# A kernel of attention and two MLPs: stores of weights behind their uses, an order made with traced durations, earlier conversions of weights

## The chip, the cores and the metric

One core of a Trainium2 chip. The time is that of one execution on the device, in microseconds (us); the median of some runs is given with the lowest and the highest. The profile is of one execution and has its own time. The engines are called PE (TensorE, the matrix products; PEld is its loading of weights), DVE (VectorE), ACT (ScalarE), POOL (GpSimd) and SP (SyncE, whose queue issues the DMAs).

## The reference

Three parts follow one another on 4 x 576 = 2304 rows of 512 numbers:

```python
# attention with a window of 128, 8 heads of 64
scores = scale * q @ k.T;  scores = where(mask, scores + bias, -1e9)
x = softmax(scores) @ v                                  # 2304 x 512
# mixing of tokens, then of channels (d_ch = 1536)
h  = maximum(xt @ w_tok1, 0) @ w_tok2;   u = x + h.T     # xt: x with rows and columns exchanged, per batch
x  = u + maximum(u @ w_ch1, 0) @ w_ch2
# normalization and a second mixing of channels (2048)
xn = (x - mu) / sqrt(var + 1e-6) * g_ln
out = x + maximum(xn @ w_ch1, 0) @ w_ch2
```

The four matrices of the channel MLPs are float64 in memory (`wa1`, `wa2` of the first, `wb1`, `wb2` of the second).

## The kernel before

The rows are 18 tiles of 128. Attention runs over the tiles, two calls a tile (`n` = 0 to 35 counts them); the token MLP is fed in between (`later()`), and so are loads of weights: while `n` lies from `W_START` on in steps of `W_STEP`, a call brings one weight of channel layer 0 (n = 24, 27, 30 and 33), and the rest of the first six come right behind attention. Then channel layer 0 and channel layer 1 follow, as 42 steps, each a layer, a chunk of tiles (tiles 0 to 7, then 16 and 17, then 8 to 15) and a pair of weight tiles of 128 x 512.

A weight is converted on the chip (`load_f64`, line 377): two DMAs of 512 KB bring it (`rh`, `rw`, line 400), ACT makes `e` (line 412), and DVE takes four instructions for it: `s` (lines 415 and 417), `m` (419), and the float32 result `w` or `y` (427). A list `uses` holds every use of a weight in turn; use number k, weight k below, has a tile `w` from a ring of `W_BUFS` = 6. A weight that is used again later, by another chunk, is stored as float32 in memory (`keep_w`, line 478; the store has line 480) and comes back by a load (line 490). Weights of layer 1 are converted ahead into two tiles `y` and stored (`stage_w`).

A product in nearly full float32 is three matmuls: each operand is split in a high part and a low part (`w1h`, `w1l`, `xh`, `xl`, and so on), of which high by high, low by high and high by low are added up. ACT makes the high part, DVE or POOL the low part (line 370). A step on eight tiles makes seven products of blocks from sums of weights and inputs (`w1_of`, `seven_products`; `st` are the sums, `b0` to `b3` the banks of PSUM, lines 971 to 973 the matmuls). ACT takes the positive part `hh` of a bank (line 906), DVE the low part `hl` (line 908), and after that the bank is free for the next step. `second` multiplies by the second weight (`w2h`, `w2l`, lines 1026 to 1028, into `acc`) and DVE adds the result to `u` (line 1031). In the first chunk `w2_of` also stores both parts of the second weight (line 945), the other chunks load them (line 950).

Nothing of this is emitted in the order in which it is written. Every operation is recorded in a `Plan` with its cost on each engine that can do it, what it reads and what it writes. `Plan.order` (line 205) then places the operations one after the other: each engine takes, of what is ready by the costs, what has the lowest rank, and an operation that DVE or POOL can do goes to the one that would end it sooner. Ranks come from the recorded order of the products. Each engine, and SP's queue of DMAs, executes what it was given in that order, so a cost changes the order of all engines and the engine of some operations. The costs are functions of the elements in a row:

```python
def dve(n, fast=False):
    return 68 + n / (1.92 if fast else 0.96)
def pool_tt(n):
    return 149 + 2.1 * n
```

Of the kernel before, what the change touches and what calls it, by code (L numbers as in the profile page):

```python
# [10 lines left out]
F32 = mybir.dt.float32  # L11
# [25 lines left out]
W_BUFS = 6  # L37
# [6 lines left out]

STAGE_RATES = {(0, 2): 2, (1, 0): 2}
WARM, WARM_NS = 10, 320
WT_SHIFT, WT_START, WT_STEP, SHIFT_AT, W_START, W_STEP = 0, 2, 1, 7, 24, 3
SIGN16, EXP16 = 0x80008000 - (1 << 32), 0x7F807F80


# [52 lines left out]
class Plan:  # L103
# [29 lines left out]
        ring.append(b)  # L133
        return b

    def op(self, cost, emit, reads=(), writes=()):
        k = len(self.ops)
        deps, behind = set(), set()
        for group, write in ((reads, False), (writes, True)):
            for x in group:  # L140
                b, key = x if isinstance(x, tuple) else (x, None)
                if not b.ops:
                    if b.pool in self.ctl:
                        b.first.add(self.ctl[b.pool])
                    for a in b.after:
                        assert a.ops, "a ring's tile is not in use yet"
                        a.closed = True
                        b.first.update(a.ops)
                deps.update(b.first)
                if b.behind:  # L150
                    behind.add(b.behind.ops[0])
                assert not getattr(b, "closed", False), f"{b.spec[2]} is used after its place was given away"
                assert write or any(w for key2, (w, _) in b.track.items() if key is None or key2 in (None, key)), \
                    f"{b.spec[2]} is read before it is written"
                b.ops.append(k)
                for key2, (ws, rs) in b.track.items():
                    if key is None or key2 is None or key == key2:
                        deps.update(ws)
                        if write:
                            deps.update(rs)  # L160
                ws, rs = b.track.setdefault(key, ([], []))
                if write:
                    if key is None:
                        b.track = {None: ([k], [])}
                    else:
                        b.track[key] = ([k], [])
                else:
                    rs.append(k)
        deps.discard(k)
        behind.discard(k)  # L170
        self.ops.append((cost, emit, deps, behind - deps, self.shift))
        return k
# [117 lines left out]
    def emit(self):  # L290
        for k in self.order():
            self.ops[k][1](self.taken[k])


def dve(n, fast=False):
    return 68 + n / (1.92 if fast else 0.96)


def act(n, psum=False, pointers=0):
    return (51 if psum else 93) + 0.833 * n + 93 * pointers  # L300


def pool_tt(n):
    return 149 + 2.1 * n


def pool_ts(n):
    return 162 + 0.833 * n


def pe(n):
# [3 lines left out]
def block_kernel(tc, qT, kT, v, wt1, wt2, wa1, wa2, wb1, wb2, g, bias, out):  # L315
    nc = tc.nc
    NF1, NF2 = FF1 // P, FF2 // P
    pl = Plan()
    buf = pl.buf

    def op(cost, emit, reads=(), writes=()):
        return pl.op(cost, (lambda e: emit()) if len(cost) == 1 else emit, reads, writes)

    ENGINE = {"DVE": nc.vector, "POOL": nc.gpsimd}

# [51 lines left out]
    def load_f64(src, k, n, dst=None, get=None):  # L377
# [29 lines left out]
        def half(x):  # L407
# [4 lines left out]
        op({"ACT": act(n)}, lambda: nc.scalar.activation(  # L412
            out=e.t[:, :n], in_=head(BF16), func=AF.Copy, scale=2.0 ** -116), [rh], [e])

        op({"DVE": dve(n // 2, True)}, lambda: nc.vector.tensor_scalar(  # L415
            half(s), half(e), 3, EXP16, ALU.logical_shift_left, ALU.bitwise_and), [e], [s])
        op({"DVE": dve(n // 2)}, lambda: nc.vector.scalar_tensor_tensor(
            out=half(s), in0=half(e), scalar=SIGN16, in1=half(s), op0=ALU.bitwise_and, op1=ALU.bitwise_or), [e], [s])
        op({"DVE": dve(n, True)}, lambda: nc.vector.tensor_scalar(
            m.t[:, :n], rw.t[:, :n, 0], 4, None, ALU.logical_shift_left), [rw], [m])  # L420
        if dst is None:
            dst = y = buf("cvt", [P, DM], F32, "y", 2)
# [1 line left out]
            def get():  # L424
                return y.t[:, :n]

        op({"DVE": dve(n)}, lambda: nc.vector.scalar_tensor_tensor(
            out=get(), in0=m.t[:, :n], scalar=2.0 ** 32, in1=s.t[:, :n], op0=ALU.add, op1=ALU.mult), [m, s], [dst])
        return dst, get

# [18 lines left out]
    uses = []  # L449
# [4 lines left out]
                if m == 1 or steps[j][1] == 0:  # L454
                    uses += [("ab"[steps[j][0]] + str(m), 2 * steps[j][3] + i) for i in range(2)]
    last_use = {x: k for k, x in enumerate(uses)}
    to_stage = [x for k, x in enumerate(uses) if x[0][0] == "b" and x not in uses[:k]]
    src = {"a1": wa1, "a2": wa2, "b1": wb1, "b2": wb2}
    wtiles, staged = [], {}
    used = [0]  # L460
# [14 lines left out]
        pl.op({"DVE": dve(DM), "POOL": pool_tt(DM)}, scale, [y, g_sb], [dst])  # L475
        return dst, get

    def keep_w(x, w, get):
        d = staged[x] = buf("dram", [P, DM], F32, f"d{len(staged)}")
        op({"DMA": 728}, lambda: nc.sync.dma_start(out=d.t, in_=get()), [w], [d])  # L480

    def load_w(upto):

        while len(wtiles) < min(upto, len(uses)):
            k = len(wtiles)
            x = uses[k]
            w = buf("wa", [P, DM], F32, "w", W_BUFS)
            wtiles.append(w)
            if x in staged:
                op({"DMA": 728}, lambda w=w, d=staged[x]: nc.sync.dma_start(out=w.t, in_=d.t), [staged[x]], [w])  # L490
            else:
                convert_w(x, w, lambda w=w: w.t)
                if last_use[x] > k:
                    keep_w(x, w, lambda w=w: w.t)

    def stage_w(n):

# [7 lines left out]
    def take_w():  # L505
        used[0] += 1
        return wtiles[used[0] - 1]


    bias_sb = buf("att", [P, 4, H, P], BF16, "bias_sb")  # L510
# [223 lines left out]
    def attention():  # L734
# [37 lines left out]
        for i in range(-1, NTILE + 1):  # L772
# [15 lines left out]
            for c in range(2):  # L788
# [13 lines left out]
                if n == SHIFT_AT:  # L802
                    shift_wt1()
                if W_START <= n < 2 * NTILE and (n - W_START) % W_STEP == 0:
                    load_w(min(W_BUFS, len(wtiles) + 1))
                later()
        return tok_later

# [92 lines left out]
    def hidden():  # L901
        return [buf("mlq", [P, CW], F32R, "h" + p, H_BUFS) for p in "hl"]

    def relu_to(h, key, c, o, go, n):
        hh, hl = h
        op({"ACT": act(n, True)}, lambda: nc.scalar.activation(  # L906
            out=hh.t[:, c], in_=go(), func=AF.Relu), [o], [(hh, key)])
        op({"DVE": dve(n)}, lambda: nc.vector.scalar_tensor_tensor(  # L908
            out=hl.t[:, c], in0=go(), scalar=0.0, in1=hh.t[:, c].bitcast(F32),
            op0=ALU.max, op1=ALU.subtract), [o, (hh, key)], [(hl, key)])  # L910

    def w1_of(s):

        f1, f2 = take_w(), take_w()
        if len(steps[s][2]) == 2:
            return [w_split("w1", W1_BUFS, x) for x in (f1, f2)]
        a, b = (buf("mlp", [P, DM], F32, "st", ST_BUFS) for _ in range(2))

        def left(x):
# [2 lines left out]
        def right(x):  # L922
            return lambda: x.t[:, HW:]
# [6 lines left out]
        minus((b, 1), right(b), f1, right(f1), (a, 0), left(a), HW)  # L930
        w2 = w_split("w1", W1_BUFS, b)
        w3 = w_split("w1", W1_BUFS, f2, right(f2), HW)
        return [(w0, 0), (w1, 0), (w2, 0), (w1, HW), (w0, HW), (w3, 0), (w2, HW)]

    parts2 = {}

    def w2_of(s):
        out = []
        layer, c, _, n = steps[s]
        for f in (2 * n, 2 * n + 1):  # L940
            if c == 0:
                x = w_split("w2", W2_BUFS, take_w())
                for p, y in zip("hl", x):
                    d = parts2[layer, f, p] = buf("dram", [P, DM], F32, f"d2{layer}{f}{p}")
                    op({"DMA": 728}, lambda d=d, y=y: nc.sync.dma_start(out=d.t, in_=y.t.bitcast(F32)), [y], [d])
            else:
                x = []
                for p in "hl":
# [234 lines left out]
```

## Time and profile before

| | us |
|---|---|
| median of 3 runs (lowest to highest) | 877.15 (875.05 to 880.37) |
| the profiled execution's own time | 875.87 |
| its span | 874.1 |
| PE, PEld busy | 838.7, 686.5 |
| DVE, ACT, POOL busy | 675.1, 367.1, 308.4 |

The span is the time from the first to the last instruction that the profile has. Busy times of different engines overlap. A wait is put down to the instruction that ended last of those that were waited for. The granted clock (PEclk) is 1.00 where PE has 2.4 GHz and 0.5 where it has 1.2. Attention and the token MLP take the first 171 us, channel layer 0 runs to some 446 us, layer 1 from there on.

### The profile page before, as it was taken

How to read it: one execution, taken by the hardware profiler on the slowest of the kernel's cores; microseconds unless marked ns; L12 is line 12 of the kernel's file. 1: busy time of each engine (PE TensorE's matmuls, PEld its weight loads, DVE VectorE, ACT ScalarE, POOL GpSimd, SP SyncE). 2: the span in 40 equal slices, each digit the busy share in tenths (PEclk: the TensorE clock that was granted, in tenths of full speed). 3: DMA queues.
4: the chain of work that ended last, by engine and by line, in shares of the span. 5: the costliest groups of instructions: out<-in, count | busy, mean ns of one | idle time of the engine just before them, and what ended most of it. 6: DMA issues, size and time to landing. Idle time of an engine off the chain costs nothing.

```text
span 874.1 us, 13184 instructions
## 1 busy us (share of the span) xinstructions
PE 838.7 (96%) x4478; PEld 686.5 (79%) x4478; DVE 675.1 (77%) x1406; ACT 367.1 (42%) x880; POOL 308.4 (35%) x327
## 2 busy tenths in 40 slices
PE   7999999969999999999998999999999999999997
PEld 6767787758887788788875787787878988888886
DVE  5787775798888999978799967899678855555554
ACT  6888765533344436223344422433344322222220
POOL 2783545363212456321223434452144322221110
PEclk9999999979999999999999999999999999999999
DMA  8688843057767789987753132885357772221112
GB/s 287 198 232 228 282 137 111 24 172 246 236 222 237 269 282 323 338 278 255 276 189 121 61 128 67 301 294 198 132 169 231 227 230 84 73 72 49 49 49 96
DMA packets 72547, 162.88 MB, mean 186 GB/s; under 512 B 8224, under 2 KB 8352, under 8 KB 72480
## 3 DMA queue, kind: packets, MB, share of 16 engines
q1 hardware_dynamic: 72000, 160.73, 55.4%
q0 software_dynamic: 480, 1.31, 0.8%
q8 instruction: 35, 0.57, 0.3%
q14 instruction: 32, 0.26, 0.1%
HBM read 129.76 MB, written 30.93 MB: 184 GB/s over the span
## 4 chain that ended last, share of the span: by engine, by line
PE 65%; DVE 11%; issue 2%; ACT 1%; POOL 0%; DVEq 0%; POOLq 0%; ACTq 0%
PE acc L1026 11%; PE acc L1028 11%; PE acc L1027 11%; PE b L971 9%; PE b L973 9%; PE b L972 9%; DVE st L824 2%; DVE u L1031 2%; DVE st L370 2%; PE b L436 1%; PE b L438 1%; DVE hl L908 1%; PE b L437 1%; PE p L832 1%; DVE s L415 1%
## 5 line engine op out<-in xcount | busy, mean ns | idle before, releaser
L1031 DVE TENSOR_TENSOR u<-acc,u 128x512 f32<-128x512 f32 x252 | 172.1, 685 | 57.3 <-PE acc L1028 55.8
L1026 PE MATMUL acc<-w2h,hh 128*128 128x512 f32 x504 | 199.2, 395 | 5.8 <-DVE u L1031 5.1
L906 ACT ACTIVATE hh<-b 128x512 fp32r<-128x512 f32 (+1 forms) x140 | 74.4, 553 | 298.2 <-PE b L973 252.9
L1028 PE MATMUL acc<-w2h,hl 128*128 128x512 f32 x504 | 196.8, 390 | 0.8 <-DVE hl L908 0.7
L1027 PE MATMUL acc<-w2l,hh 128*128 128x512 f32 x504 | 196.6, 390 | 0.0
L971 PE MATMUL b<-xh,w1h 128*128 128x512 f32 x392 | 155.7, 397 | 8.6 <-DVE hl L908 5.0
L973 PE MATMUL b<-xh,w1l 128*128 128x512 f32 x392 | 154.1, 393 | 0.6 <-POOL w1l L370 0.6
L972 PE MATMUL b<-xl,w1h 128*128 128x512 f32 x392 | 154.1, 393 | 0.0
L908 DVE SCALAR_TENSOR_TENSOR hl<-b,hh 128x512 fp32r<-128x512 f32 (+1 forms) x140 | 85.6, 630 | 53.2 <-ACT hh L906 52.9
L370 POOL TENSOR_TENSOR w1l<-w,w1h 128x512 fp32r<-128x512 f32 (+1 forms) x47 | 60.8, 1296 | 184.5 <-ACT w1h L357 184.3
L1026 PEld LDWEIGHTS acc<-w2h,hh 128*128 128x128 f32 x504 | 94.7, 188 | 29.6 <-DVE u L1031 10.3
L1028 PEld LDWEIGHTS acc<-w2h,hl 128*128 128x128 f32 x504 | 94.6, 188 | 22.3 <-DVE hl L908 2.4
L1027 PEld LDWEIGHTS acc<-w2l,hh 128*128 128x128 f32 x504 | 94.8, 188 | 18.1
L971 PEld LDWEIGHTS b<-xh,w1h 128*128 128x128 f32 x392 | 74.5, 190 | 26.5 <-DVE hl L908 5.4
L973 PEld LDWEIGHTS b<-xh,w1l 128*128 128x128 f32 x392 | 74.5, 190 | 17.1 <-POOL w1l L370 1.1
L972 PEld LDWEIGHTS b<-xl,w1h 128*128 128x128 f32 x392 | 74.6, 190 | 15.2
L370 POOL TENSOR_TENSOR w1l<-st,w1h 128x512 fp32r<-128x512 f32 x30 | 39.8, 1328 | 125.7 <-ACT w1h L357 118.1
L412 ACT ACTIVATE e<-rh 128x512 bf16<-128x512 bf16 (+2 forms) x65 | 41.2, 634 | 66.0 <-DMA rh<-wb 38.0
L635 ACT ACTIVATE pr<-t,mn 128x128 f32<-128x128 f32 x144 | 55.8, 391 | 19.2 <-DVE mn L626 18.8
L652 POOL TENSOR_SCALAR_AFFINE_SELECT pf<-pf 128x512 f32<-128x512 f32 x64 | 42.8, 671 | 34.1 <-ACT pf L357 32.1
L370 DVE TENSOR_TENSOR b<-b,p 128x512 f32<-128x512 f32 x56 | 38.8, 694 | 18.2 <-PE b L973 18.2
L370 POOL TENSOR_TENSOR xl<-st,xh 128x512 fp32r<-128x512 f32 x23 | 30.0, 1307 | 51.8 <-ACT xh L357 51.7
(118 smaller groups left out, 1371.3 us busy)
## 6 DMA issues: line engine op xcount, KB each, us to landing
w<-d SPq DMA_DIRECT2D x82, 256.0 KB, 3.2
rw<-wb SPq DMA_DIRECT2D x32, 512.0 KB, 4.7
rh<-wb SPq DMA_DIRECT2D x32, 512.0 KB, 4.9
rw<-wa SPq DMA_DIRECT2D x24, 512.0 KB, 4.4
rh<-wa SPq DMA_DIRECT2D x24, 512.0 KB, 4.4
d<-y SPq DMA_DIRECT2D x26, 256.0 KB, 3.9
keys<-kT SPq DMA_DIRECT2D x18, 256.0 KB, 4.1
q<-qT SPq DMA_DIRECT2D x18, 256.0 KB, 4.5
```

The lines of the kernel that those rows point to most:

```text
L370: pl.op({e: cost[e] for e in on}, lambda e: ENGINE[e].tensor_tensor(get(), ga(), gb(), alu), [*several(a), *several(b), *also], several(dst))
L635: op({"ACT": 580}, lambda m=m: nc.scalar.activation(out=pr.t[:, m], in_=t.t[:, m], func=AF.Exp, bias=mn.t[:, m:m + 1], scale=-1.0, accum_o ...
L652: op({"POOL": 630}, lambda a=a: nc.gpsimd.affine_select(pf.t[:, a], pf.t[:, 1], [[0, 4], [1 - 2 * a, P]], (ALU.is_ge, ALU.is_gt)[a], 0.0, ...
L906: op({"ACT": act(n, True)}, lambda: nc.scalar.activation(out=hh.t[:, c], in_=go(), func=AF.Relu), [o], [(hh, key)])
L908: op({"DVE": dve(n)}, lambda: nc.vector.scalar_tensor_tensor(out=hl.t[:, c], in0=go(), scalar=0.0, in1=hh.t[:, c].bitcast(F32), op0=ALU.ma ...
L971: nc.tensor.matmul(g.t, wh.t[:, w], xh.t, start=start and k == 0, stop=False, skip_group_check=True)
L972: nc.tensor.matmul(g.t, wh.t[:, w], xl.t, start=False, stop=False, skip_group_check=True)
L973: nc.tensor.matmul(g.t, wl.t[:, w], xh.t, start=False, stop=stop and k == 1, skip_group_check=True)
L1026: nc.tensor.matmul(o.t, hh.t[:, c:c + P], wh.t, start=j == 0, stop=False)
L1027: nc.tensor.matmul(o.t, hh.t[:, c:c + P], wl.t, start=False, stop=False)
L1028: nc.tensor.matmul(o.t, hl.t[:, c:c + P], wh.t, start=False, stop=j == 1)
L1031: op({"DVE": dve(DM)}, lambda o=o, i=i: nc.vector.tensor_tensor(u[i].t, o.t, u[i].t, ALU.add), [o], [u[i]])
```

## The change

Four things are done. The constants `W_START`, `W_STEP` go from 24, 3 to 18, 2: nine calls in attention (n = 18, 20, to 34) instead of four; the first six load a weight each, the other three stage one (weights 6, 7 and 8, converted into a tile `y`, stored as `d0`, `d1`, `d2` and loaded back later). The store of a loaded weight is recorded no longer with its conversion but behind the splits that use it (`keep_taken`), and it may not stand ahead of the last of these in the order (`behind`). The stores of the parts of the second weight are put behind the last `hl` that was recorded before (`mark`). And the costs of DVE, ACT and POOL are raised; those of the four DVE instructions of a conversion have a factor of 1.3 besides. The rest of the diff passes `behind` on.

```diff
-WT_SHIFT, WT_START, WT_STEP, SHIFT_AT, W_START, W_STEP = 0, 2, 1, 7, 24, 3
+WT_SHIFT, WT_START, WT_STEP, SHIFT_AT, W_START, W_STEP = 0, 2, 1, 7, 18, 2
...
-    def op(self, cost, emit, reads=(), writes=()):
+    def op(self, cost, emit, reads=(), writes=(), behind=()):
         k = len(self.ops)
-        deps, behind = set(), set()
+        deps, behind = set(behind), set()
...
 def dve(n, fast=False):
-    return 68 + n / (1.92 if fast else 0.96)
+    return 150 + n / (1.92 if fast else 0.97)
...
 def act(n, psum=False, pointers=0):
-    return (51 if psum else 93) + 0.833 * n + 93 * pointers
+    return 170 + (0.82 if psum else 0.9) * n + 93 * pointers
...
 def pool_tt(n):
-    return 149 + 2.1 * n
+    return 150 + 2.4 * n
...
 def pool_ts(n):
-    return 162 + 0.833 * n
+    return 200 + 0.95 * n
...
-        op({"DVE": dve(n // 2, True)}, lambda: nc.vector.tensor_scalar(
+        op({"DVE": 1.3 * dve(n // 2, True)}, lambda: nc.vector.tensor_scalar(
             half(s), half(e), 3, EXP16, ALU.logical_shift_left, ALU.bitwise_and), [e], [s])
...
-    to_stage = [x for k, x in enumerate(uses) if x[0][0] == "b" and x not in uses[:k]]
+    to_stage = [x for k, x in enumerate(uses) if x not in uses[:k]]
...
-    def keep_w(x, w, get):
+    def keep_w(x, w, get, behind=()):
         d = staged[x] = buf("dram", [P, DM], F32, f"d{len(staged)}")
-        op({"DMA": 728}, lambda: nc.sync.dma_start(out=d.t, in_=get()), [w], [d])
+        op({"DMA": 728}, lambda: nc.sync.dma_start(out=d.t, in_=get()), [w], [d], behind)
...
                 convert_w(x, w, lambda w=w: w.t)
-                if last_use[x] > k:
-                    keep_w(x, w, lambda w=w: w.t)
...
+    def keep_taken(n):
+
+        for k in range(used[0] - n, used[0]):
+            if uses[k] not in staged and last_use[uses[k]] > k:
+                keep_w(uses[k], wtiles[k], lambda w=wtiles[k]: w.t, [len(pl.ops) - 1])
...
                 if W_START <= n < 2 * NTILE and (n - W_START) % W_STEP == 0:
-                    load_w(min(W_BUFS, len(wtiles) + 1))
+                    if len(wtiles) < W_BUFS:
+                        load_w(len(wtiles) + 1)
+                    else:
+                        stage_w(1)
...
-        op({"DVE": dve(n)}, lambda: nc.vector.scalar_tensor_tensor(
+        mark[0] = op({"DVE": dve(n)}, lambda: nc.vector.scalar_tensor_tensor(
...
         w3 = w_split("w1", W1_BUFS, f2, right(f2), HW)
+        keep_taken(2)
...
         layer, c, _, n = steps[s]
+        last = [mark[0]]
...
-                    op({"DMA": 728}, lambda d=d, y=y: nc.sync.dma_start(out=d.t, in_=y.t.bitcast(F32)), [y], [d])
+                    op({"DMA": 728}, lambda d=d, y=y: nc.sync.dma_start(out=d.t, in_=y.t.bitcast(F32)), [y], [d], last)
```

Lines up to 490 keep their numbers; behind that line 908 becomes 918, 945 becomes 959, 971 to 973 become 985 to 987, 1026 to 1028 become 1040 to 1042 and 1031 becomes 1045. In the order that comes out, 36 operations go from DVE to POOL. The numbers behind a name below tell one instance of a buffer from another.

On DVE, the last instructions ahead of the first `hl` of channel layer 0 (`hl` frees bank `b0`; `e`, `s`, `m`, `rw` belong to conversions), before:

```order
L415 TENSOR_SCALAR s_2468<-e_2215 128x256
L419 TENSOR_SCALAR m_2476<-rw_2012 128x512
L417 SCALAR_TENSOR_TENSOR s_2468<-e_2215,s_2468 128x256
L427 SCALAR_TENSOR_TENSOR w_2484<-m_2476,s_2162 128x512
L370 TENSOR_TENSOR xl51_2492<-st_2411,xh51_2423 128x512
L415 TENSOR_SCALAR s_2504<-e_2486 128x256
L419 TENSOR_SCALAR m_2506<-rw_2038 128x512
L417 SCALAR_TENSOR_TENSOR s_2504<-e_2486,s_2504 128x256
L370 TENSOR_TENSOR w1l_2521<-w_1626,w1h_2501 128x512
L908 SCALAR_TENSOR_TENSOR hl_2525<-b0_2426,hh_2508 128x512
L427 SCALAR_TENSOR_TENSOR w_2529<-m_2506,s_2468 128x512
```

Seven of the nine rows ahead of `hl` belong to conversions. After, the same place:

```order
L370 TENSOR_TENSOR w1l_2455<-st_2428,w1h_2450 128x512
L417 SCALAR_TENSOR_TENSOR s_2400<-e_2388,s_2400 128x256
L419 TENSOR_SCALAR m_2472<-rw_2153 128x512
L370 TENSOR_TENSOR xl41_2478<-p0_2381,xh41_2402 128x512
L370 TENSOR_TENSOR w1l_2490<-st_2444,w1h_2461 128x512
L370 TENSOR_TENSOR w1l_2494<-w_1626,w1h_2474 128x256
L427 SCALAR_TENSOR_TENSOR y_2502<-m_2472,s_2345 128x512
L370 TENSOR_TENSOR b3_2277<-b1_2273,p5_2496 128x512
L415 TENSOR_SCALAR s_2519<-e_2480 128x256
L419 TENSOR_SCALAR m_2524<-rw_2230 128x512
L417 SCALAR_TENSOR_TENSOR s_2519<-e_2480,s_2519 128x256
L918 SCALAR_TENSOR_TENSOR hl_2539<-b0_2437,hh_2521 128x512
```

Six of the eleven rows ahead of `hl` belong to conversions: one that ends in `y`, a staged weight, and the first steps of the next; splits of weights and inputs stand between them.

On PE, the products around the second one that goes into bank `b0` (which that `hl` frees), before:

```order
L971 MATMUL b1_2336<-xh10_2312,w1h_2437 128x512
L972 MATMUL b1_2336<-xl10_2322,w1h_2437 128x512
L973 MATMUL b1_2336<-xh10_2312,w1l_2453 128x512
L971 MATMUL b1_2336<-xh11_2413,w1h_2437 128x512
L972 MATMUL b1_2336<-xl11_2421,w1h_2437 128x512
L973 MATMUL b1_2336<-xh11_2413,w1l_2453 128x512
L971 MATMUL b0_2535<-xh00_2259,w1h_2501 128x512
L972 MATMUL b0_2535<-xl00_2269,w1h_2501 128x512
L973 MATMUL b0_2535<-xh00_2259,w1l_2521 128x512
```

The new `b0` comes behind the product of the second of the four weights (`w1h_2437`). After:

```order
L985 MATMUL b1_2273<-xh50_2340,w1h_2474 128x512
L986 MATMUL b1_2273<-xl50_2351,w1h_2474 128x512
L987 MATMUL b1_2273<-xh50_2340,w1l_2494 128x512
L985 MATMUL b1_2273<-xh51_2430,w1h_2474 128x512
L986 MATMUL b1_2273<-xl51_2448,w1h_2474 128x512
L987 MATMUL b1_2273<-xh51_2430,w1l_2494 128x512
L985 MATMUL b0_2566<-xh00_2235,w1h_2534 128x512
L986 MATMUL b0_2566<-xl00_2244,w1h_2534 128x512
L987 MATMUL b0_2566<-xh00_2235,w1l_2543 128x512
```

It now comes behind the product of the last one, two products later.

On SP, the DMAs from the same place on (line 400 brings a weight to be converted, line 480 stores a converted one, line 945, now 959, a part of a second weight, line 490 loads a stored weight), before:

```order
L400 DMA rh_2224<-wa2 128x4096
L945 DMA d200h_2442<-w2h_2435 128x512
L480 DMA d4_2462<-w_2455 128x512
L945 DMA d201h_2481<-w2h_2464 128x512
L400 DMA rw_2488<-wa2 128x4096
L400 DMA rh_2513<-wa1 128x4096
L400 DMA rw_2531<-wa1 128x4096
L480 DMA d5_2549<-w_2484 128x512
L945 DMA d200l_2562<-w2l_2511 128x512
L945 DMA d201l_2569<-w2l_2527 128x512
```

The stores stand among the loads as their weights are converted. After:

```order
L480 DMA d3_2512<-w_1528 128x512
L480 DMA d2_2532<-y_2502 128x512
L400 DMA rw_2537<-wa1 128x4096
L480 DMA d4_2573<-w_1626 128x512
L400 DMA rh_2575<-wa2 128x4096
L490 DMA w_2583<-d0_2212 128x512
L490 DMA w_2612<-d1_2361 128x512
L959 DMA d200h_2622<-w2h_2435 128x512
L480 DMA d5_2632<-w_1909 128x512
L959 DMA d201h_2643<-w2h_2453 128x512
L959 DMA d200l_2646<-w2l_2476 128x512
L959 DMA d201l_2656<-w2l_2498 128x512
```

The stores `d3`, `d4`, `d5` come behind the splits, those of the parts behind them, and `d2` is one of the three staged weights, of which `d0` and `d1` are loaded back here.

## Rows read from the trace of the kernel before

**Rows 1.** The page's first part: busy us (share) x instructions of each engine.

```profile
PE 838.7 (96%) x4478; PEld 686.5 (79%) x4478; DVE 675.1 (77%) x1406; ACT 367.1 (42%) x880; POOL 308.4 (35%) x327
```

**Rows 2.** Busy time by stretch: from:to, length, then the columns of the header.

```profile
core 0: us, PE busy (x) PEld busy (x) DVE busy (x) ACT busy (x) POOL busy (x), PEclk, DMA share, GB/s
0.00:50.00 50.00, 44.43 (x398) 35.19 (x400) 32.82 (x160) 39.00 (x147) 25.12 (x49) 1.00 0.72 239
50.00:100.00 50.00, 45.96 (x445) 35.86 (x443) 39.45 (x171) 39.47 (x147) 28.69 (x45) 1.00 0.85 245
...
150.00:171.00 21.00, 21.00 (x110) 17.32 (x110) 13.86 (x22) 9.23 (x17) 4.92 (x4) 1.00 0.07 25
171.00:199.00 28.00, 18.86 (x68) 14.05 (x67) 26.33 (x38) 13.72 (x26) 17.37 (x15) 0.82 0.50 163
...
250.00:300.00 50.00, 48.81 (x217) 39.58 (x216) 44.34 (x72) 21.96 (x41) 15.26 (x13) 1.00 0.67 226
350.00:400.00 50.00, 48.52 (x215) 40.14 (x215) 42.48 (x88) 15.16 (x29) 14.52 (x15) 1.00 0.88 302
446.00:483.00 37.00, 32.62 (x140) 23.79 (x139) 36.87 (x63) 18.08 (x33) 15.90 (x14) 1.00 0.36 121
542.00:551.00 9.00, 7.88 (x31) 5.21 (x31) 9.00 (x14) 1.18 (x2) 5.76 (x6) 1.00 0.66 222
642.00:680.00 38.00, 35.45 (x225) 31.27 (x224) 33.73 (x65) 18.07 (x37) 16.68 (x13) 1.00 0.70 225
700.00:750.00 50.00, 50.00 (x222) 41.42 (x221) 27.51 (x41) 10.62 (x21) 11.99 (x13) 1.00 0.41 135
```

**Rows 3.** Waits, 172 to 202 us: waiter <- releaser, total us, times, longest.

```profile
PE b L971 <- DVE hl L908: 5.0, 1, 5.0
```

**Rows 4.** Timeline of PE: start, us, line, output <- inputs [idle before <- releaser].

```profile
178.55 0.79 PE L971 MATMUL b<-xh,w1h 128*128 128x512 f32 x1 [0.61 <-ACT b L357]
...
184.73 0.39 PE L973 MATMUL b<-xh,w1l 128*128 128x512 f32 x1
190.08 0.80 PE L971 MATMUL b<-xh,w1h 128*128 128x512 f32 x1 [4.96 <-DVE hl L908]
190.67 0.63 PE L972 MATMUL b<-xl,w1h 128*128 128x512 f32 x1
```

**Rows 5.** Timeline of DVE, and of POOL at 474, in the same columns.

```profile
182.54 1.50 DVE L417 SCALAR_TENSOR_TENSOR s<-e,s 128x256 int32<-128x256 int32 x1
183.97 1.78 DVE L427 SCALAR_TENSOR_TENSOR w<-m,s 128x512 f32<-128x512 uint32 x1
...
189.35 0.67 DVE L908 SCALAR_TENSOR_TENSOR hl<-b,hh 128x512 fp32r<-128x512 f32 x1
...
196.22 0.43 DVE L417 SCALAR_TENSOR_TENSOR s<-e,s 128x256 int32<-128x256 int32 x1
...
473.86 3.56 DVE L824 TENSOR_SCALAR st<-u,mv,rstd 128x128 f32<-128x128 f32 x4
474.13 2.52 POOL L370 TENSOR_TENSOR w2l<-w,w2h 128x512 fp32r<-128x512 f32 x2
```

**Rows 6.** DVE's conversions, 171 to 199.5 us: xcount | busy us, mean ns.

```profile
L427 DVE SCALAR_TENSOR_TENSOR w<-m,s 128x512 f32<-128x512 uint32 x4 | 4.3, 1086 | 0.0
L419 DVE TENSOR_SCALAR m<-rw 128x512 uint32<-128x512 uint32 x3 | 2.8, 949 | 0.0
L417 DVE SCALAR_TENSOR_TENSOR s<-e,s 128x256 int32<-128x256 int32 x3 | 2.3, 779 | 0.0
L415 DVE TENSOR_SCALAR s<-e 128x256 int32<-128x256 int32 x3 | 1.9, 638 | 0.0
```

**Rows 7.** Waits of SP's queue over the span, columns as in rows 3.

```profile
SPq L400 <- ACT e L412: 63.4, 34, 9.5
SPq L480 <- DVE w L427: 28.1, 11, 4.9
```

**Rows 8.** Groups by form over the span: xcount | busy, mean ns | idle before.

```profile
L370 POOL TENSOR_TENSOR w1l<-w,w1h 128x512 fp32r<-128x512 f32 x43 | 56.6, 1319 | 182.9 <-ACT w1h L357 182.9
L824 DVE TENSOR_SCALAR st<-u,mv,rstd 128x128 f32<-128x128 f32 x72 | 34.5, 526 | 0.0
L370 DVE TENSOR_TENSOR w1l<-w,w1h 128x256 fp32r<-128x256 f32 x24 | 22.9, 953 | 3.3 <-ACT w1h L357 3.1
```

**Rows 9.** DMA issues over the span: KB each, median us from issue to landing.

```profile
d<-w SPq DMA_DIRECT2D x18, 256.0 KB, 3.1
```

More of the change, by code (lines that the diff above doesn't have):

```diff
@@ L319, in block_kernel, with op @@
     buf = pl.buf
-    def op(cost, emit, reads=(), writes=()):
-        return pl.op(cost, (lambda e: emit()) if len(cost) == 1 else emit, reads, writes)
+    def op(cost, emit, reads=(), writes=(), behind=()):
+        return pl.op(cost, (lambda e: emit()) if len(cost) == 1 else emit, reads, writes, behind)
     ENGINE = {"DVE": nc.vector, "POOL": nc.gpsimd}
@@ L413, in load_f64 @@
             out=e.t[:, :n], in_=head(BF16), func=AF.Copy, scale=2.0 ** -116), [rh], [e])
-        op({"DVE": dve(n // 2, True)}, lambda: nc.vector.tensor_scalar(
+        op({"DVE": 1.3 * dve(n // 2, True)}, lambda: nc.vector.tensor_scalar(
             half(s), half(e), 3, EXP16, ALU.logical_shift_left, ALU.bitwise_and), [e], [s])
-        op({"DVE": dve(n // 2)}, lambda: nc.vector.scalar_tensor_tensor(
+        op({"DVE": 1.3 * dve(n // 2)}, lambda: nc.vector.scalar_tensor_tensor(
             out=half(s), in0=half(e), scalar=SIGN16, in1=half(s), op0=ALU.bitwise_and, op1=ALU.bitwise_or), [e], [s])
-        op({"DVE": dve(n, True)}, lambda: nc.vector.tensor_scalar(
+        op({"DVE": 1.3 * dve(n, True)}, lambda: nc.vector.tensor_scalar(
             m.t[:, :n], rw.t[:, :n, 0], 4, None, ALU.logical_shift_left), [rw], [m])
@@ L425, in get @@
                 return y.t[:, :n]
-        op({"DVE": dve(n)}, lambda: nc.vector.scalar_tensor_tensor(
+        op({"DVE": 1.3 * dve(n)}, lambda: nc.vector.scalar_tensor_tensor(
             out=get(), in0=m.t[:, :n], scalar=2.0 ** 32, in1=s.t[:, :n], op0=ALU.add, op1=ALU.mult), [m, s], [dst])
@@ L902, in hidden @@
         return [buf("mlq", [P, CW], F32R, "h" + p, H_BUFS) for p in "hl"]
+    mark = [0]
     def relu_to(h, key, c, o, go, n):
@@ L907, in relu_to @@
             out=hh.t[:, c], in_=go(), func=AF.Relu), [o], [(hh, key)])
-        op({"DVE": dve(n)}, lambda: nc.vector.scalar_tensor_tensor(
+        mark[0] = op({"DVE": dve(n)}, lambda: nc.vector.scalar_tensor_tensor(
             out=hl.t[:, c], in0=go(), scalar=0.0, in1=hh.t[:, c].bitcast(F32),
@@ L915, in w1_of @@
         if len(steps[s][2]) == 2:
-            return [w_split("w1", W1_BUFS, x) for x in (f1, f2)]
+            out = [w_split("w1", W1_BUFS, x) for x in (f1, f2)]
+            keep_taken(2)
+            return out
         a, b = (buf("mlp", [P, DM], F32, "st", ST_BUFS) for _ in range(2))
@@ L932, in w1_of @@
         w3 = w_split("w1", W1_BUFS, f2, right(f2), HW)
+        keep_taken(2)
         return [(w0, 0), (w1, 0), (w2, 0), (w1, HW), (w0, HW), (w3, 0), (w2, HW)]
```

## The prediction

> **What bounds the kernel now.** I read the busy line of the page first: TensorE (PE) is busy 96% of the span [rows 1], so all that an edit of the order can win is PE's idle time and the time that it runs at the lower clock. The table of stretches then says where that is [rows 2]. In 700 to 750 us PE is busy 50.00 of 50 us and does 222 matmuls, 0.225 us each: this is PE's own pace, and no order beats it. The stretch that stands out is 171 to 199 us, the step from attention and the token MLP into the products of channel layer 0: PE is busy 18.86 of 28.00 us, with a granted clock of 0.82, and VectorE (DVE) 26.33 of 28.00. The table of waits names the largest piece: PE waits once, 5.0 us, for `hl` of line 908, which DVE makes [rows 3]. The timeline of PE shows it before the matmul of 190.08, and the lower of the two clock levels (1.2 of 2.4 GHz) after it: 0.63 us for a matmul of 512 columns that takes 0.39 at 184.73 [rows 4]. DVE is not waiting in that time. It is at conversions of weights, one after another, and `hl` stands behind them: 1.50, 1.78 us and so on, then `hl` at 189.35 [rows 5]. Of its 38 instructions there 13 belong to conversions and take 4.3 + 2.8 + 2.3 + 1.9 = 11.3 us [rows 6]. So the first weights are converted too late, and DVE is the bound of this stretch.
>
> Smaller losses of the same look, DVE full and PE short: 446 to 483 us (idle 4.38 us, DVE 36.87 of 37), 542 to 551 (1.12, DVE 9.00 of 9), 642 to 680 (2.55), 250 to 300 and 350 to 400 (1.19 and 1.48) [rows 2]. The first 100 us lose 5.57 and 4.04 us in attention, to many small waits [rows 2].
>
> **The change part by part.** *Earlier conversions.* Before, six weights of channel layer 0 have their conversions ahead of its first product, and three more finish among the products. After, the nine calls put eight ahead of it and the ninth just behind it. Between the last transposes ahead of the layer's input and the fourth `hl`, DVE has 37 instructions before (12 of conversions) and 26 after (6). Eleven less at this stretch's mean, 26.33/38 = 0.69 us, are 7.6 us. The bounds: at the undisturbed length of the second step of a conversion, 0.43 us at 196.22 [rows 5], they are 4.7 us; at most PE gets back all its idle time, 9.14 us, and the lower clock, 19 matmuls (11 from 178.55, 8 from 190.08) that are 0.20 us further apart, 3.8 us: 12.9 us. I take **-7**, near the mean of this very stretch; two products more also stand ahead of the one that waits for `hl`, which speaks for the gain not being less. What is late next is PE's own input, `xl`, which DVE makes too.
>
> *What the moved conversions cost where they land.* DVE gets seven more conversion instructions in 150 to 171 us, and others earlier in attention. They come to 3 us at 0.43, and to 6 at this stretch's 0.69 to 0.95. DVE is busy 13.86 of 21 there, with 7.1 free [rows 2]; PE is busy all the time and covers them. If that cover is gone, up to 3 us come out at the end; **+1**. In the first 100 us the order of attention changes a little as well, since all costs do; PE has 9.6 us idle there to win or lose in, and nothing in the trace says which: 0, with -3 to +3. The three stores of staged weights and their loads are 6 DMAs of 256 KB where the queues move 25 GB/s (150 to 171), so nothing waits for their bytes.
>
> *The new costs.* They raise ScalarE and DVE instructions to what the trace has, and POOL's less, so the planner hands 36 more tensor operations to POOL. Most are sums and `w1l`; one takes 1.32 us on POOL and 0.95 on DVE [rows 8]. In the stretches where DVE is full it loses 4 of 70 instructions (446 to 483), 4 of 17 (542 to 551) and 10 of 69 (642 to 680). At 36.87/63 = 0.59 us the first is 2.3 us of 4.38: **-2** (0 to -4.4). The second, 4 x 0.64 = 2.6, is more than PE's 1.12 idle: **-1** (0 to -1.1). The third: **-1.5** (0 to -2.5). For 250 to 400, of 2.67 idle us, **-1** (0 to -2.7). Their lower ends are at 0 because POOL's result can come as late as DVE's did.
>
> *Stores behind their uses.* The ten stores of loaded weights now follow the splits, the stores of `w2` parts follow the relu. In the queue of SyncE (SP) this takes away waits in front of loads: the queue stands 28.1 us in 11 waits at line 480 [rows 7]. No engine is shown waiting for it in 171 to 199, so I count no gain. A price is new: a store that is later keeps its tile of the ring of six longer, and the conversion that writes the tile next must wait until it has landed, 3.1 us after its issue [rows 9]. By the order seven conversions (weights 9, 16, 17, 20, 21, 24, 25) write a tile whose store stands only three to five products ahead, 4.1 to 6.8 us of PE time. If SP issues the store at once, none waits. At worst all wait out a whole landing, 7 x 3.1 = 21.7 us of DVE. A wait at line 480 has a mean of 28.1/11 = 2.6 us; I take one such: **+2.5**. Queued behind a waiting conversion on DVE are `hl` and the additions of line 1031, for which PE waits.
>
> Sum: -7 + 1 - 2 - 1 - 1.5 - 1 + 2.5 = **-9.0 us**. From the profiled execution's 875.87 (span 874.1 and 1.8 around it) that is 866.9. It lies 1.3 below the median, 877.15 (875.05 to 880.37); from the median it is **868**.
>
> **The rivals.** *POOL holds DVE up, no change.* Between 473.86 and 477.4 four small DVE instructions take 3.56 us, 0.89 each, while POOL runs two tensor operations of 1.26 us [rows 5]; the mean of this form over the kernel is 0.53 [rows 8]. So an operation given to POOL isn't free for DVE. If each of the 36 holds DVE for its whole 1.32 us, that is 47.5 us, more than the 36 x 0.95 = 34 us saved. Then the 5.5 us of the DVE-full stretches are gone and half of the 7: -9 + 5.5 + 3.5 = 0, **877**. Against it: most DVE instructions beside POOL's are not stretched at all, as those that read PSUM, `hl` at 189.35 with 0.67 us [rows 5]. The Trainium skill ("SBUF — State Buffer", Who interferes with whom) says that an instruction of DVE with two inputs in SBUF, or in a mode with two ports, shares a port pair with GpSimd's reads, and that whoever issues first blocks the other entirely. By that rule every such instruction that meets a POOL operation waits it out, which is this rival; the trace agrees in kind at 473.86, and shows less than a whole block for most.
>
> *The ring's stores are late, slower.* If SP stands at the head of its queue while one of the seven stores is due, the conversion waits longer than one landing. At 6 us each, 42 us of DVE; DVE has 5.7 and 7.5 us free in 50 [rows 2], some 20 in the 150 us that these lie in, so PE loses 22. With the other terms (-11.5) that is +10.5: **888**. The point from which it decides: 7 x d - 20 = 11.5, d = 4.5 us; the store would have to be issued 5.5 to 8.2 us late (4.5 plus the lead of 4.1 to 6.8 less 3.1). SP does stand for as long as 9.5 us, at a load of line 400 [rows 7], but its mean is 63.4/34 = 1.9, and all seven would have to meet it.
>
> *Only a part is done.* Nine calls stand where the change speaks of ten, and the ninth ends behind the first product; three weights go through DRAM and come back by loads that were not there. If the loads, behind other DMAs, are what PE then waits for, about half of the 7 is lost and the stretches give half: -4.5, **873**.
>
> **How the numbers follow.** Forecast, 862 to 872: 0.50. Part only, 870 to 875: 0.15, of which 0.09 is beyond 0.5%. No change: 0.18, with 0.01 faster. Late stores, or an order of attention that loses as much: 0.17, 882 to 890. A measurement of this kernel can tell about 0.5% from no change, 4.4 us: faster is below 872.8. That makes 0.60 faster, 0.23 the same, 0.17 slower. For eight in ten the range leaves out the deeper gain (all bounds at their best, 855) and most of the late stores: 859 to 880.
>
> **What would show it.** Right: the stretch behind the last token-MLP matmul is some 7 us shorter, its granted clock nearer 1, the wait of 5.0 for `hl` under 2, and DVE has about 27 instructions there instead of 38. POOL is busy about 355 us instead of 308, DVE 650 instead of 675. PE's idle time in 446 to 483 is about half. Wrong: new waits of DVE for a store `d<-w`; small DVE instructions longer on average than now; PE waiting for POOL's `w1l` or for `w<-d`. The forecast fails if `hl` is late for another reason than the conversions, as then nothing of the -7 comes.

## The result, and the profile after

The changed kernel takes 863.77 us (median of 4, 863.58 to 864.12), the kernel before beside it 877.99 (875.05 to 880.37): a ratio of 0.984, with a 95% interval of 0.981 to 0.987, 14.2 us. The two profiled executions are 12.3 us apart, 875.87 and 863.61. The forecast was 868, its range 859 to 880.

The page's busy line, and the stretches in the columns of [rows 2], of the kernel after:

```profile
PE 835.6 (97%) x4478; PEld 688.2 (80%) x4478; DVE 650.4 (75%) x1370; ACT 366.9 (43%) x880; POOL 349.8 (41%) x363
```

```profile
50.00:100.00 50.00, 48.87 (x460) 38.70 (x456) 37.85 (x167) 41.90 (x154) 30.57 (x49) 1.00 0.81 236
...
150.00:171.00 21.00, 19.14 (x99) 15.36 (x97) 18.79 (x31) 12.91 (x24) 9.19 (x7) 1.00 0.38 133
171.00:199.00 28.00, 24.18 (x94) 18.59 (x95) 21.89 (x30) 12.14 (x24) 16.80 (x15) 0.82 0.55 188
...
450.00:500.00 50.00, 45.43 (x201) 36.74 (x200) 47.38 (x95) 19.76 (x36) 25.20 (x22) 0.97 0.40 121
```

Two things differ at a glance. In 50 to 100 us, in attention, PE is busy 48.87 us where it was 45.96. In 171 to 199 it does 94 matmuls where it did 68, but the granted clock is 0.82 again. The stretches no longer hold the same work, so the table below counts work. It lists when PE starts the last matmul of the token MLP, and then the n-th matmul of the channel layers (those into `b` and `acc`, in the order of the timeline; those of 256 columns count half):

| | before | after | gained so far | gained here |
|---|---|---|---|---|
| last of the token MLP | 170.1 | 166.9 | 3.2 | 3.2 |
| n = 100 | 209.7 | 202.0 | 7.7 | 4.5 |
| n = 1100 | 446.3 | 438.8 | 7.5 | -0.2 |
| n = 1250 | 491.5 | 483.0 | 8.5 | 1.0 |
| n = 1500 | 550.5 | 539.7 | 10.8 | 2.3 |
| n = 1800 | 619.7 | 607.7 | 12.0 | 1.2 |
| last | 869.7 | 857.9 | 11.8 | -0.2 |

The waits of PE over the whole span, of the kernel after, in the columns of [rows 3]:

```profile
PE p L839 <- DVE st L831: 5.4, 4, 3.1
PE b L987 <- DVE w1l L370: 2.1, 1, 2.1
...
PE ps_t L646 <- ACT pf L357: 1.4, 2, 0.7
PE acc L1040 <- DVE u L1045: 1.3, 2, 1.0
...
PE b L985 <- DVE hl L918: 1.0, 2, 0.8
```

and three of the kernel before:

```profile
PE acc L1026 <- DVE u L1031: 5.1, 10, 1.1
PE ps_t L642 <- ACT pf L357: 5.1, 5, 1.4
PE b L971 <- DVE hl L908: 5.0, 1, 5.0
```

The wait of 5.0 us for `hl` [rows 3] is gone. So are most waits of attention's transposes (`ps_t`) for ScalarE's `pf`, and most of those of the second products (`acc`) for DVE's additions to `u`. New are 2.1 us for `w1l`, which has taken the place of `hl` in the step into channel layer 0, and 3.1 us for the normalized tile `st` at the start of layer 1. The latter in the timelines of DVE, POOL and PE:

```profile
458.41 4.06 DVE L831 TENSOR_SCALAR st<-u,mv,rstd 128x128 f32<-128x128 f32 x4
...
465.54 1.11 DVE L831 TENSOR_SCALAR st<-u,mv,rstd 128x128 f32<-128x128 f32 x4
...
458.64 1.30 POOL L370 TENSOR_TENSOR xl<-st,xh 128x512 fp32r<-128x512 f32 x1 [1.74 <-ACT xh L357]
459.89 2.50 POOL L370 TENSOR_TENSOR w2l<-w,w2h 128x512 fp32r<-128x512 f32 x2
...
465.93 1.25 PE L839 MATMUL p<-ident,st 128*128 128x128 f32 x4 [3.08 <-DVE st L831]
```

Four such instructions take 1.11 us where POOL is idle for most of that time, and 4.06 beside three operations of POOL.

### The profile page after: what moved, and what is told of

The parts are those of the page before. It is cut to its first block, busy times and chain, and to the rows that moved or that the text cites. A ratio compares the mean times of both kernels' runs of the same rounds, so it can differ in the third digit from the quotient of the medians.

```text
span 861.9 us, 13152 instructions
## 1 busy us (share of the span) xinstructions
PE 835.6 (97%) x4478; PEld 688.2 (80%) x4478; DVE 650.4 (75%) x1370; ACT 366.9 (43%) x880; POOL 349.8 (41%) x363
## 4 chain that ended last, share of the span: by engine, by line
PE 65%; DVE 8%; issue 1%; DMA 1%; ACT 1%; SPq 0%; DVEq 0%; ACTq 0%
PE acc L1040 12%; PE acc L1042 12%; PE acc L1041 12%; PE b L985 9%; PE b L987 9%; PE b L986 9%; DVE st L831 2%; DVE st L370 1%; DVE u L1045 1%; PE b L436 1%; PE b L438 1%; PE b L437 1%; PE p L839 1%; DVE xl L370 1%; DVE hl L918 1%
## 5 line engine op out<-in xcount | busy, mean ns | idle before, releaser
L1045 DVE TENSOR_TENSOR u<-acc,u 128x512 f32<-128x512 f32 x252 | 172.0, 686 | 59.8 <-PE acc L1042 56.6
L370 POOL TENSOR_TENSOR w1l<-w,w1h 128x512 fp32r<-128x512 f32 (+1 forms) x55 | 71.1, 1292 | 164.9 <-ACT w1h L357 164.4
L370 POOL TENSOR_TENSOR w1l<-st,w1h 128x512 fp32r<-128x512 f32 x37 | 49.4, 1336 | 113.9 <-ACT w1h L357 107.9
L357 ACT ACTIVATE w1h<-w 128x512 fp32r<-128x512 f32 x84 | 46.6, 555 | 4.4 <-PE b L986 2.5
```

What stands on the lines that cost most here:

```text
L357: nc.scalar.activation(out=get(), in_=gsrc(), func=AF.Copy, scale=scale)
L370: pl.op({e: cost[e] for e in on}, lambda e: ENGINE[e].tensor_tensor(get(), ga(), gb(), alu), [*several(a), *several(b), *also], several(dst))
L1045: op({"DVE": dve(DM)}, lambda o=o, i=i: nc.vector.tensor_tensor(u[i].t, o.t, u[i].t, ALU.add), [o], [u[i]])
```

## The experiments

### Each part alone, and two together

The costs alone are the lines of `dve`, `act`, `pool_tt`, `pool_ts` and the four factors of the diff. The earlier conversions alone:

```diff
-WT_SHIFT, WT_START, WT_STEP, SHIFT_AT, W_START, W_STEP = 0, 2, 1, 7, 24, 3
+WT_SHIFT, WT_START, WT_STEP, SHIFT_AT, W_START, W_STEP = 0, 2, 1, 7, 18, 2
...
-    to_stage = [x for k, x in enumerate(uses) if x[0][0] == "b" and x not in uses[:k]]
+    to_stage = [x for k, x in enumerate(uses) if x not in uses[:k]]
...
-                    load_w(min(W_BUFS, len(wtiles) + 1))
+                    if len(wtiles) < W_BUFS:
+                        load_w(len(wtiles) + 1)
+                    else:
+                        stage_w(1)
```

The later stores alone are `keep_taken`, `behind` and `mark`.

Costs alone. 

> The kernel before with the new costs alone (all of them, the factor 1.3 too); four loads of weights in attention and the stores where they were. Three theories on the 14 us that the whole change gains. Conversions: the earlier conversions bring some 7, at the step into channel layer 0, and the costs the rest, so this run is 6 to 7 us faster than before (about 871), with PE's wait of 5 us for hl still there, as 12 instructions of conversions still stand on VectorE between the first product and the fourth hl. Costs: the order made with traced durations brings nearly all of it, 865 or 866. Stores: what SyncE's queue no longer waits for brings most, and this run gains 2 at most (875).

Earlier conversions alone. 

> The kernel before with the earlier conversions alone: nine calls in attention, each weight stored right behind its conversion, old costs. No conversion is left on VectorE between the first product and the fourth hl (12 before). Conversions: 7 us faster (870), the wait for hl under 2 us, and no gain elsewhere. Costs: 2 us at most, since the old costs make VectorE's instructions shorter than they are, so the conversions hold up attention by what they free later. Stores: 2 at most.

Later stores alone. 

> The kernel before with the later stores alone, those of the loaded weights and those of the parts of the second weight. The order shifts by itself: 5 instructions of conversions instead of 12 stand on VectorE between the first product and the fourth hl. Conversions: part of that step's gain comes without any earlier conversion, 2 to 4 us (874), less what waits for late stores cost (0 to 2.5). Costs: no change (877). Stores: 8 us or more (869).

Costs and earlier conversions. 

> The whole change without the later stores: each loaded weight is stored right behind its conversion, the parts of the second weight right behind their splits. Conversions: as fast as the whole change, 864, or 1 to 2.5 us faster, since no conversion waits for a late store. Costs: 864 to 866. Stores: most of the gain is gone, 870 or more.

Costs and later stores, run at the end. 

> The whole change without the earlier conversions (four calls in attention from n = 24 on in steps of 3, costs and stores as in the whole change). By the order 8 instructions of conversions stand on VectorE between the first product and the fourth hl, 12 with the costs alone and 6 with everything. Theory, one place for all three: each of the three parts takes conversions away from ahead of hl, and any two do what all three do, so the run takes 863 to 865. Rival, the earlier conversions are needed: it takes 867, as with the costs alone.

| | us (median) | ratio to before (95%) | step into layer 0, us |
|---|---|---|---|
| before | 877 to 879 | | 39.6 |
| costs | 867.26 | 0.988 (0.985 to 0.991) | 37.7 |
| early | 874.68 | 0.996 (0.994 to 0.998) | 37.4 |
| stores | 870.41 | 0.993 (0.990 to 0.995) | 35.4 |
| costs, early | 864.12 | 0.985 (0.982 to 0.989) | 35.8 |
| costs, stores | 863.15 | 0.985 (0.981 to 0.988) | 35.2 |
| all three | 863.77 | 0.984 (0.981 to 0.987) | 35.1 |

The last column is n = 100 less the last matmul of the token MLP, from the profiled execution. In `early` and `stores` 8 of the 24 transposes of `u` that the other rows have ahead of that matmul come behind it, so these two steps hold about 1 us more. The single gains, 11.1, 3.7 and 8.0 us, come to 22.8, and the whole is 14.2: the parts have a gain in common. With the costs, either of the other two does what both do. The pair without the costs was not run.

The theory of conversions had the largest share in the wrong part: the earlier conversions bring 3.7 us alone, not 7, and the costs 11, not 6 or 7. It was right that the costs leave the wait for `hl`; of the costs alone:

```profile
PE p L832 <- DVE st L824: 5.4, 4, 3.1
PE b L971 <- DVE hl L908: 5.1, 2, 5.0
```

The theory of costs came nearest to that run (865 or 866), but 3 of the 14 us are left to the others. The theory of stores came near for the later stores alone (869 for 870.41) and failed with the costs alone (875) and without the stores (870 or more). The earlier conversions alone fit none of the three (870, or 2 us at most). The theory of one place had the time of the last pair right (863 to 865), but its reason does not hold for the costs, which leave conversions and the wait where they were.

In every run of the table that clears the wait for `hl`, another wait stands in the step instead. The longest ones from 160 to 202 us, of `early`, `stores`, `costs, early` and `costs, stores`:

```profile
PE b L974 <- ACT b L357: 3.6, 1, 3.6
PE b L982 <- ACT b L357: 3.3, 1, 3.3
PE b L974 <- ACT w1h L357: 7.1, 2, 5.8
PE p L836 <- DVE xl L370: 4.0, 1, 4.0
```

With all three parts it is the 2.1 us for `w1l`. That is where the gains in the step overlap: with two parts or three it is 35 to 36 us long, whatever cleared `hl`.

Attention belongs to the costs. `ps_t` waits 5.1 us, in 5 waits, with the earlier conversions alone and with the later stores alone, as before, and 1.4 in 2 in every run with the new costs. The old cost of ScalarE's copy out of PSUM was 51 + 0.833 x 512 = 477 ns, the trace has 591; the new one is 590, and the planner puts other matmuls ahead of some transposes. That it is this cost, and not another of the new ones, was not tried alone.

### Order or engines

Each of the 330 operations with a choice was bound to the engine of one plan while the other plan's costs set the order:

```diff
+        pinned, opts = iter(PINNED), []
+        for op in ops:
+            opts.append(list(op[0]))
+            if len(opts[-1]) > 1:
+                first = next(pinned)
+                opts[-1] = [e for e in opts[-1] if e[0] == first]
```

New costs, old engines. 

> The kernel before with the new costs, but each of the 330 operations that ScalarE, VectorE or GpSimd could do stays on the engine that it had before (a table fixes it): no operation moves to GpSimd, only the order is new. Theory order: what the costs gain (11 us) comes from the order, above all in attention (PE's idle time in 50 to 100 us was 4.0 before and 1.1 with the new costs), and this run is 7 us or more faster than before (871 or less). Theory engines: it comes from VectorE's 37 operations less, and this run gains 3 us at most (875).

Old costs, new engines. 

> The kernel before with its old costs, but each of the 330 operations goes to the engine that the new costs gave it: 37 more on GpSimd, the order made with the old costs. Theory order: 3 us faster at most (875), and it may be slower, since 13 instructions of conversions stand between the first product and the fourth hl. Theory engines: 8 us faster or more (869 or less).

They took 869.62 us (0.990, 0.987 to 0.994) and 874.60 (0.997, 0.996 to 0.999). So the order brings 7.7 us of the costs' 11.1. The 37 operations more on POOL bring 2.7 with the old costs; what they add to the new order, 2.4 us by the two medians, is not clear of noise, as the intervals of the two runs overlap. Theory order holds on the total, and the operations on POOL do not eat what they free on DVE.

The two gain at different places. The last matmul of the token MLP starts at 167.4 us with the new order and at 170.4 with the new engines (170.1 before), and `ps_t` waits 1.4 and 5.1 us: attention is a matter of the order. The step into layer 0 is 39.3 us long with the new order and 35.8 with the new engines. The wait of 5.0 us for `hl` is gone in both, but with the new order PE waits 3.8 us for `b` from DVE in the step instead.

### The two kinds of stores

The stores of the loaded weights alone leave out `mark`; the stores of the parts alone leave out `keep_taken`.

> Of the later stores, those of the loaded weights alone (the parts of the second weights are stored as before). The conversions of weights 6 to 8 come out of the planner behind the first hl instead of ahead of it (products 234 to 241 instead of 228 to 231), and 5 instructions of conversions stand between the first product and the fourth hl instead of 12. Theory late conversions: this brings all that the later stores gave (8 us, 870), and the other half nothing. Theory queue: what SyncE's queue waits for at the stores of the parts (57 us in 13 waits) is what was gained, and this run gains 2 at most (876).

> Of the later stores, those of the parts of the second weights alone. The conversions stay where they were before (12 instructions between the first product and the fourth hl). Theory late conversions: no change (877). Theory queue: 6 us or more faster (872 or less).

They took 875.90 us (0.998, 0.996 to 1.000) and 879.48 (1.002, 1.001 to 1.004). Both theories fail on the total: neither half brings what both bring, 8.0. The step shows what each does. With the loaded weights' stores it is 35.4 us long, as with both; with the parts' stores it is 39.7, and PE waits for `hl` for 4.7 us. So the loaded weights' stores do take the conversions from ahead of `hl`, by putting them behind it: the ring's tile is free later, so the planner places the conversion later. The prediction feared this dependence as a wait of DVE; here the planner answers it with a later place, and the step gains. Where the half loses it again, from the waits of PE and the timeline of DVE with the loaded weights' stores:

```profile
PE acc L1035 <- DVE hl L912: 5.0, 3, 4.0
```

```profile
301.90 0.69 DVE L427 SCALAR_TENSOR_TENSOR y<-m,s 128x512 f32<-128x512 uint32 x1
302.63 1.63 DVE L472 TENSOR_TENSOR y<-y,g_sb 128x512 f32<-128x512 f32 x1
304.19 0.68 DVE L370 TENSOR_TENSOR w1l<-w,w1h 128x512 fp32r<-128x512 f32 x1
304.79 1.94 DVE L912 SCALAR_TENSOR_TENSOR hl<-b,hh 128x512 fp32r<-128x512 f32 x4
```

It is the pattern of [rows 5] at another place: a conversion, of a weight of layer 1, ahead of an `hl` that PE needs. Any edit shifts the whole order and meets such places or not. Why the parts' stores remove this one when they come on top was not tried.

### Fewer calls

```diff
-W_START, W_STEP = ..., 18, 2
+W_START, W_STEP = ..., 20, 2
```

> The whole change with eight calls in attention instead of nine (from n = 20 on in steps of 2; two weights are staged). By the order 2 instructions of conversions stand on VectorE between the first product and the fourth hl, where the whole change has 6; 21 instructions altogether in both. Theory, what stands ahead of hl counts: the step into channel layer 0 gets 1 to 2.5 us shorter and the run takes 862. Theory, what is ready early counts: one weight less is converted ahead of the first product, so the run is 1 to 3 us slower, 865 to 867.

It took 864.85 us (863.33 to 866.12), on a chip where the whole change was not timed; the step is 34.4 us long instead of 35.1, and at n = 200 the gain is gone again (226.8 us against 226.3). The end is 1.1 us above the whole change, within the spread of its own four executions. The run doesn't tell the two theories apart; it shows that the ninth conversion is worth little.

### The normalizations on ScalarE, and an address

```diff
+    shift = buf("const", [P, NTILE], F32, "shift")
...
-                op({"DVE": 250}, lambda i=i, j=j, g=get[j]: nc.vector.tensor_scalar(
-                    x.t[:, j], g(), mv.t[:, i, 0:1], rstd.t[:, i:i + 1], ALU.subtract, ALU.mult),
-                    [u[i], (mv, i), (rstd, i)], [(x, j)])
+                def norm(i=i, j=j, g=get[j]):
+                    nc.scalar.activation(out=x.t[:, j], in_=g(), func=AF.Identity,
+                                         bias=shift.t[:, i:i + 1], scale=rstd.t[:, i:i + 1])
+                op({"ACT": act(P, pointers=1)}, norm, [u[i], (mv, i), (rstd, i), (shift, i)], [(x, j)])
...
```

> The whole change, with the 72 normalizations of layer 1 (st from u, mv, rstd, line 831) on ScalarE instead of VectorE, as one activation with a scale and an added number per row; the latter costs one small instruction more per chunk. At the start of layer 1 four of these took 4.06 us on VectorE while GpSimd ran three operations, and 1.11 us a little later without them; PE waited 5.4 us for them in all. Theory, GpSimd holds VectorE up: that wait goes, PE's idle time in 450 to 500 us falls from 4.6 to under 2 and the run gains 2 to 4 us (860 to 862). Rival, VectorE is simply full there: the wait passes to another of its results (hl, xl or u), and the run gains less than 1 us, 863 or more.

It took 866.55 us (865.52 to 867.71), 2.8 more than the whole change. That is against the first theory, and in the rival's range (863 or more) but not for its reason. What the first one says of the place is there: the wait for `st` is gone, and the stretch 450 to 500 has PE busy 48.32 us instead of 45.43. What it lost it lost everywhere else, where nothing waits:

```profile
450.00:500.00 50.00, 48.32 (x217) 38.57 (x216) 43.43 (x81) 26.00 (x53) 24.59 (x23) 1.00 0.37 122
...
700.00:750.00 50.00, 50.00 (x218) 40.61 (x217) 26.19 (x41) 12.98 (x26) 10.90 (x11) 1.00 0.33 105
```

In 700 to 750 us PE is busy all the time at the full granted clock and does 218 matmuls instead of 222. In 700 to 800 us the starts of successive matmuls of 512 columns are 231.5 ns apart on the mean instead of 226.7, and from 200 us to the end 231.6 instead of 227.1. The products into `b` lose more (233.6 ns in 700 to 800 us) than those into `acc` (229.7).

```diff
-    even = buf("even", [P, EVEN], F32, "even")
+    even = shift = buf("even", [P, EVEN], F32, "even")
...
-    shift = buf("const", [P, NTILE], F32, "shift")
```

> The same as the run with the normalizations on ScalarE, instruction for instruction and in the same order, but the added number per row (18 columns of float32, 72 bytes a partition) lies in the tile even, which nothing else uses, instead of in a new buffer, so that every other buffer has the address that it has in the whole change. With the new buffer PE had less idle time than the whole change (17.0 us instead of 22.7), but its matmuls of 512 columns followed each other in 231.7 ns instead of 226.7 from 200 us on, and 1,600 of them took that back. Theory, addresses: the 72 bytes moved the buffers that PE reads, the pace goes back to 226.7 and the run takes 856 to 860, faster than the whole change. Rival, the work on ScalarE or the fuller PE is what slows it: the pace stays above 230 and the run takes 865 to 867.

It took **854.87 us** (854.27 to 856.96), 0.974 of before (0.971 to 0.977), 8.9 us below the whole change: the fastest kernel here. Theory addresses holds, with a time 1 us below its range. Its stretches:

```profile
450.00:500.00 50.00, 48.29 (x220) 39.07 (x219) 42.63 (x80) 26.38 (x55) 23.76 (x22) 1.00 0.37 121
700.00:750.00 50.00, 50.00 (x223) 41.39 (x221) 27.24 (x43) 11.04 (x23) 12.86 (x14) 1.00 0.25 82
```

The pace is back (223 matmuls, 226.7 ns) and the idle time of layer 1's start stays away. The same instructions in the same order differ by 11.7 us through 72 bytes of one buffer's place (the two ran on different chips, where the kernel before took 878.95 and 877.65). Which operand of PE minds, and at which addresses, was not tried.

## Why the prediction was right, step by step

**The bound.** Right: most of what was won are waits of PE. Its idle time fell from 31.3 to 22.7 us (the sums of the gaps in its timeline), 8.6 of the 12.3 between the profiled executions.

**Earlier conversions, -7 + 1.** The wait for `hl` went as the rows said, and DVE's instructions in the step (171 to 199 us before, 167 to 192 after) fell from 38 to 30, those of conversions from 13 to 8. The step got 4.5 us shorter, not 6. The term was mis-sized: it valued the instructions saved at DVE's mean as if all of it went to PE, while 2.1 of the 5.0 us came back as a wait for `w1l` (not for `xl`, which the prediction named as next). Its sign of a granted clock nearer to 1 did not come: PE has the lower level for 10.2 us of the step before (176.4 to 183.2 and 190.1 to 193.5) and for 10.2 after (172.0 to 182.2, among waits of 0.8 to 2.1 us). The part was also wrongly tied to the earlier conversions: by the runs each of the three parts shortens this step, and the whole change without the earlier conversions takes 863.15 us, no longer than with them.

**Attention, 0.** The step that failed: "nothing in the trace says which". 3.2 us were gained, and 4.3 with costs and earlier conversions, whose profiled execution kept the full clock at the start (the last section). The waits of `ps_t` for ScalarE were in the trace, 5.1 us, and so was the duration of ScalarE's copy, 114 ns above its cost. The runs tie these waits to the order that the new costs make; that this one cost explains them is likely and not shown. New costs of an engine should have been held against the waits for that engine, stage by stage.

**The new costs elsewhere, -5.5.** From n = 100 on 4.1 us were gained in the profiled executions: 1.0 at the start of layer 1 for 2 forecast, 2.3 to n = 1500 for 1, 1.2 to n = 1800 for none, and none in 250 to 400 and at 642 to 680, where 1 and 1.5 were expected. The sum was fair, the places were not: PE's idle time at the start of layer 1 did not halve (4.4 of 37 us before, 4.7 from 438 to 475 after), and the largest wait that went here is one that the prediction gives no price of its own, 5.1 us for `u`, now 1.3.

**Late stores, +2.5.** Nothing of it came: with and without them the time is 863.77 and 864.12, and DVE has no wait for a store in the trace of the changed kernel. The term took one wait of SP's mean length, and none came.

So the sum, -9.0, stands against 11.8 in the table of matmuls (12.3 between the profiled executions): attention's 3.2 were forecast as 0 and the 2.5 of the stores did not come, while the step and the places behind it gave 1.5 and 1.4 less than forecast. That the wait for `hl` goes and shortens the step is shown. That errors of both signs left the sum so near was luck, and so were the small terms, which came at other places.

**The rivals.** POOL rose to 349.8 us and DVE fell to 650.4, as forecast (355, 650). That POOL holds DVE up is true at one place, the 4.06 us above, and moving these instructions away took the wait for `st` with it; over the kernel the operations given to POOL bring 2.7 us (with the old costs) instead of costing 5.5. The Trainium skill ("SBUF — State Buffer", Who interferes with whom) says that an instruction of DVE in a mode with two ports and one of GpSimd shut each other out: the one that issues first has the shared ports for its whole length. The traces agree for `st`: 0.28 us each with POOL mostly idle, 1.02 beside POOL; which mode the instructions had they do not show. The ring's stores cost nothing. That only a part is done was wrong too: PE waits for none of the new loads, and nine calls, eight or four are worth the same beside the new costs and the later stores.

## What to carry to other kernels

Correct the planner's costs from a trace first: here that alone brought 11 of 14 us, most of it by the order and not by the engines chosen. Gains of edits that clear the same place do not add up, so run them alone and in pairs before crediting one, and look each time for the wait that takes the place of the one that went. When PE shows no idle time and is yet slower, count matmuls in a stretch in which nothing waits, before and after: a pace that differs there is not a matter of order.

## What the hardware showed that was not expected

A buffer of 72 bytes a partition, put among others, made PE's matmuls of 512 columns 2.1% slower (231.5 ns against 226.7 in 700 to 800 us) at a granted clock of 1.00; on the same chip, in the same session, another kernel without it (eight calls) had 226.7.

The kernel before varies by 5 us between four executions (by 7 in all sessions), the changed one by 0.5 in its four. A place where executions differ is the start, 15 to 20 us, in the kernel before and with the parts' stores alone (a profiled execution of 881.35 us):

```profile
15.00:20.00 5.00, 4.59 (x44) 3.25 (x42) 4.35 (x23) 3.75 (x15) 2.58 (x5) 1.00 0.93 320
```

```profile
15.00:20.00 5.00, 4.89 (x37) 3.47 (x34) 2.65 (x14) 2.08 (x6) 1.50 (x3) 0.69 0.61 204
```

After the many small waits there PE sometimes has the lower clock for some microseconds, and sometimes not. The profiled execution of the changed kernel has it for 3.4 us, from 18.4 to 21.8, that of the kernel before at no time in attention; at half the pace, an estimate, that is 1.7 us. That the 2 us between medians and profiled executions (14.2 and 12.3) come from this fits the rows, but the other executions have no trace.
